# End pass over Wo by even and odd heads, eight projections in halves, two loads held back, in a two-layer memory-attention and gated-MLP kernel

## The chip, the cores and the metric

The kernel runs on one core of a Trainium2 chip. The metric is the device time of one execution in microseconds. A core has a TensorE (PE) for matmuls, a VectorE (DVE), a ScalarE (ACT), a GpSimd (POOL) and a SyncE (SP), each with its own instruction queue, which it works through in order. DMAs are issued from the queues of SP and POOL here. Matmul results go to PSUM banks of 512 fp32 columns on 128 partitions.

## The reference, cut to what matters

```python
x = A_x                                                  # (1, 2048, 512)
x = x + _A_ref(_layernorm(x), A_mem0, A_Wq, A_Wk, A_Wv, A_Wo, 32)
x = x + _B_ref(_layernorm(x), B_w_in, B_w_sp, B_b_sp, B_w_out)
x = x + _A_ref(_layernorm(x), A_mem0, A_Wq, A_Wk, A_Wv, A_Wo, 32)
x = x + _B_ref(_layernorm(x), B_w_in, B_w_sp, B_b_sp, B_w_out)

def _A_ref(x, mem0, Wq, Wk, Wv, Wo, seg_len):            # 64 segments of 32 tokens, 32 heads of 128
    mem, outs = mem0, []
    for s in range(n_seg):
        h = concatenate([mem, x[:, 32*s:32*s+32]])       # 8 memory rows + 32 tokens
        q, k, v = h @ Wq, h @ Wk, h @ Wv
        p = softmax(where(mask, q @ k.T * scale, -1e9))
        o = (p @ v) @ Wo                                 # summed over the heads
        mem = o[:, :8]                                   # into the next segment
        outs.append(o[:, 8:])
    return concatenate(outs)

def _B_ref(x, w_in, w_sp, b_sp, w_out):                  # w_in (512, 1376), w_sp (2048, 2048)
    z = gelu(x @ w_in)
    z1, z2 = z[..., :688], layernorm(z[..., 688:])
    g = w_sp @ z2 + b_sp
    return (z1 * g) @ w_out
```

## The kernel before, in words

Weights and activations are bf16, sums fp32. Each of the two layers is an `a_block` (attention) followed by a `b_block` (gated MLP). Rows of x are handled in 16 tiles of 128.

**a_block.** 64 segments run one after the other, since the memory rows of one feed the next. `segment(s, ...)` computes Q, K and V of the segment's 32 rows. A matmul uses 32 of the array's 128 columns, so four of them, at column strips 0, 32, 64 and 96 (`tile_position`), run side by side (L689, L879). Scores (L903), probabilities times V (L929), and sums over keys (L975, L984) follow; then `wo_pass` (L746) applies Wo to give the next memory rows. `uT` holds the attention result that goes into Wo for the next pass: results of a segment's first 24 tokens are put through Wo one segment later together with the next segment's memory rows. The last 8 tokens of each segment (`oB`) go through Wo in groups of 16 segments, later, in `y_part`/`wo_last` (L759, matmuls of 512 columns, four strips), and are added into `yB` by VectorE (L776). Each segment calls back: `fill()` for such extra TensorE work, `spare1` and `spare2` for row work in the middle, `tail` at the end.

The number of TensorE instructions in a segment is kept constant by splitting some projections in two (`pads_of`): `PE_PAGE = 256` and three pages per segment.

**The last segments (60 to 63).** The MLP's weights w_in are loaded into the `front` buffer in four slices (`load_w(kt)`, L169 and L170, two DMAs of 176 KB each, issued from POOL). `front` also holds attention buffers of even row tiles, so a slice may be loaded once TensorE has read those. Rows that are finished are joined with x (`y_load` L220 and L222, `y_add` L226, `y_stats`, `y_norm` L236), stored as x (`xd`) and, normalised, as `xb_d`; `load_rows` (L177) brings them back transposed for the MLP. Tile 11's rows are loaded into `rowsB` in segment 63's `spare1`.

**The end pass.** After segment 63, the last segment's tokens (`uT`) and the last 8 tokens of tile 15's four segments (`oB`) still have to go through Wo: the loop at L1111 to L1116. For each of 32 heads, four matmuls of 256 columns: strips 0 and 1 take `uT` with the lower and upper half of Wo's columns, strips 2 and 3 the same with `oB`. ACT copies the bank's 256 columns (L1118), and four DMAs store it (L1123, L1125), two from SP and two from POOL. ACT then loads the Gelu table.

**b_block.** `project(tt)` for 16 row tiles (12 matmuls each in three column chunks, L282, into `pz`, of which there are two), Gelu on ACT (L283), row statistics on VectorE (L286); meanwhile rows of tiles 12 to 15 are joined (`late_sum`, `late_norm`). Then `gate` (L383) over w_sp, `product`, `finish` (L426).

PE, DVE and ACT run in the order in which the code is written (`manual_schedule`, which in `b_block` includes SP). In `a_block`, the instructions of POOL and SP are put in order by a scheduler that places each by when its inputs are ready; a load that nothing holds back can so be placed ahead of the point where it is written. Before, slice 2 of w_in is written in segment 62's `tail` and issued at the start of segment 61, and tile 11's o_d rows are written in segment 63's `spare1` and issued in segment 61.

Of the kernel before, what the change touches and what calls it, by code (L numbers as in the profile page):

```python
# [8 lines left out]
F32 = mybir.dt.float32  # L9
ACT = mybir.ActivationFunctionType  # L10
ALU = mybir.AluOpType
# [3 lines left out]
P = 128  # L15
DM = 512
KT = 4
H = 32
DH = 128
HD = H * DH  # L20
M = 8
SEG = 32
LN_EPS = 1e-5
FF = 1376
FH = 688
# [214 lines left out]
def b_block(tc, c, rows, front, xd, MV_out, RS_out, w_sp, w_out, S, first, ahead, wo, out_final=None):  # L240

    nc = tc.nc
    NT = S // P
    ident_bf = c["ident_bf"]
    with ExitStack() as ctx:
# [17 lines left out]
        def z(tt, lo=0, hi=FF):  # L263
            return zs[tt >= 6][:, tt - 6 * (tt >= 6), lo:hi]
# [12 lines left out]
        def project(tt):  # L277
            pz = big.tile([P, 1536], F32, name="pz")
            xnT = front.xnT[tt // 2][:, :, P * (tt % 2):P * (tt % 2) + P]
            for c0, c1 in ((0, 512), (512, 1024), (1024, FF)):  # L280
                for kt in range(KT):
                    nc.tensor.matmul(pz[:, c0:c1], lhsT=xnT[:, kt, :], rhs=w_in_sb[:, kt, c0:c1], start=(kt == 0), stop=(kt == KT - 1))  # L282
            nc.scalar.activation(out=z(tt), in_=pz[:, 0:FF], func=ACT.Gelu_apprx_tanh)  # L283
            st = zp.tile([P, 2, nc.vector.BN_STATS_DIM], F32, name="bnst2")
            for k in range(2):
                nc.vector.bn_stats(out=st[:, k, :], in_=z(tt, 344 * k, 344 * k + 344))  # L286
            nc.vector.bn_aggr(out=slot(tt), in_=st[:])

        def slot(tt):
            group = next(g for g in GROUPS if tt in g)  # L290
            if group not in where:
                where[group] = (zp.tile([P, 8, 2], F32, name="mv"), zp.tile([P, 8], F32, name="rs"), zp.tile([P, 8], F32, name="nb"))
            return where[group][0][:, group.index(tt), :]
# [31 lines left out]
        for k in range(4):  # L325
            if k == 0:
                x, o = (rows.pool.tile([P, DM], F32, name=name)[:] for name in ("y_x", "y_o"))
                spare = x.bitcast(BF16)
            elif k == 1:
                x, o = (gp.tile([P, DM], F32, name="xo")[:] for _ in range(2))  # L330
            else:
                wl = wsp_pools[k - 1].tile([P, 2, DM], F32, name="wspL", tag="wspT")
                x, o = wl[:, 0, :], wl[:, 1, :]
# [38 lines left out]
        n = 6 * P  # L372
# [260 lines left out]
def a_block(tc, c, rows, front, MV_in, RS_in, MV_out, RS_out, ahead, wo, S, first):  # L633
    nc = tc.nc
    NSEG = S // SEG
    NB = S // P
# [3 lines left out]
    with ExitStack() as ctx:  # L640
# [13 lines left out]
        wk = ctx.enter_context(tc.tile_pool(name="a_work", bufs=2))  # L654
# [44 lines left out]
        o_d, maskM = rows.o_d, c["maskM"]  # L699
# [7 lines left out]
        rowsB = rowp.tile([P, 2, 512], BF16, name="rowsB", bufs=1)  # L707
        copies, turns, adds = [], [], []

        def run(todo):  # L710
            while todo:
                todo.pop(0)()
# [50 lines left out]
        def y_part(G, q, last=False):  # L763

            groups = [oBs[G][:, :, 32 * g:32 * g + 32] for g in range(4)]
            if last:
                parts = [[(groups[g], 8 * q + k) for g in range(3)] + [(groups[q], 24 + k)] for k in range(8)]
            else:
                parts = [[(groups[g], 8 * q + k) for g in range(4)] for k in range(8)]
            pwB = accA.tile([P, DM], F32, name="pwB")  # L770
            for k, _ in enumerate(wo_last(parts, pwB)):
                if k + 1 in (1, 2, 4):
                    yield

            def add(lo, n, src):
                nc.vector.tensor_tensor(out=yB[G][lo:lo + n, :], in0=pwB[src:src + n, :], in1=yB[G][lo:lo + n, :], op=ALU.add)  # L776

            def out():
                n = 96 if last else P
                if q == 0:  # L780
                    yB[G] = wk.tile([P, DM], F32, name="yB", bufs=1)
                    nc.vector.tensor_copy(yB[G][0:n, :], pwB[0:n, :])
                else:
                    add(0, n, 0)
                if last:
                    if q == 2:
                        store_last(G, 0, 64, nc.sync)
                    add(32 * q, 32, 96)
                    if q == 2:
                        store_last(G, 64, 96, nc.sync)  # L790
                elif q == 3 and G < NB // 4 - 2:
                    stores.append(lambda: store_last(G, 0, P, nc.sync))
                elif q == 3:
                    store_last(G, 0, P, nc.sync)

            adds.append(out)
            yield
# [240 lines left out]
        def values(units):  # L1038
            for n in (3, 1):
                for _ in range(n):  # L1040
                    next(units)
                run(copies)
                yield

        for s in range(NSEG):
            tb, j4 = s // 4, s % 4
            if j4 == 0:
                q = tb % 4
                more = y_part(tb // 4 - 1, q) if tb > 3 else iter(())
            if first and s == 0:  # L1050
                more = values(units)
            if j4 > 0 and tb == NB - 1:
                more = y_part(tb // 4, j4 - 1, last=True)
            elif j4 == 1:
                more = b_units(tb + 1)
            if j4 == 1 and tb + 2 < NB:
                rows.load(tb + 2, first, nc.sync)

            def spare1():
                if first and s == 1:  # L1060
                    ln_turn(1)
                if ys:
                    rows.y_add(ys[0], first, nc.vector, nc.sync)
                elif stores:
                    last = yB[tb // 4 - 1][:, 0:1]
                    nc.vector.tensor_copy(last, last)
                    run(stores)
                if j4 == 3 and tb + 2 < NB:
                    rows.apply(tb + 2, MV_in, RS_in, first=first)
                if s == NSEG - 1:  # L1070
                    rows.y_load(due[0], first, nc.sync, rows.pool.tile([P, DM], F32, name="y_x")[:],
                                rowsB[:].rearrange("p a n -> p (a n)").bitcast(F32))()

            def spare2():
                if first and s == 0:
                    rows.apply(1, MV_in, RS_in, first=True)
                if first and s == 8:
                    c["cast_bsp"] = c["load_bsp"]()
                if first and s == 12:
                    c["cast_bsp"]()  # L1080
                if ys:
                    y_stats(ys[0])
                if j4 == 2 and tb + 2 < NB and first:
                    _stats(nc, rows.pool, rows.xs[tb + 2], MV_in[:, tb + 2, :])
                    copies.append(lambda: _rstd_act(nc, RS_in[:, tb + 2:tb + 3], MV_in[:, tb + 2, 1:2], c))

            def tail():
                if j4 == 0 and tb + 1 < NB and not (first and s == 0):
                    ln_turn(tb + 1)
                if tb == NB - 1:  # L1090
                    front.load_w(j4)
                    if j4 > 0:
                        front.load_rows(j4 - 1)
                if ys:
                    y_norm(ys.pop(0), nc.sync)
                if tb % 4 == 3 and j4 == (tb + 1 < NB) and tb > 4:
                    due.extend(range(tb - 7, tb - 3))

                if due and (j4 != 3 or tb + 2 >= NB) and s < NSEG - 1:
                    ys.append(due.pop(0))  # L1100
                    rows.y_load(ys[0], first, nc.sync)()

            segment(s, lambda: next(more, None), spare1, spare2, tail)
# [4 lines left out]
        y_norm(due[0], nc.sync)  # L1108
        ends = (uT[NSEG % 2], oBs[NB // 4 - 1][:, :, 96:128])
        pw = accB.tile([P, 512], F32, name="pw")  # L1110
        for h in range(H):  # L1111
            n = h // 8 * 8 + 2 * (h % 4) + h // 4 % 2
            for k in range(4):
                nc.tensor.matmul(pw[32 * k:32 * k + 32, 0:256], lhsT=ends[k // 2][:, n, :],
                                 rhs=wo.head(h).rearrange("p (kt g el) -> p g kt el", kt=4, g=4)[:, k % 2 * 2:k % 2 * 2 + 2],
                                 start=(h == 0), stop=(h == H - 1), tile_position=(0, 32 * k))  # L1116
        o_sb = wk.tile([P, 256], F32, name="o_end", bufs=1)
        nc.scalar.copy(o_sb[:], pw[:, 0:256])  # L1118
        for k in range(4):
            c0 = 256 * (k % 2)  # L1120
            eng = nc.sync if k % 2 else nc.gpsimd
            if k < 2:
                eng.dma_start(o_d[SEG * NSEG - 24:SEG * NSEG, c0:c0 + 256], o_sb[32 * k + 8:32 * k + 32, :])  # L1123
            else:
                eng.dma_start(o_d[M + P * NB - P:M + P * NB, c0:c0 + 256].rearrange("(j r) c -> j r c", j=4)[:, 24:32, :], o_sb[32 * k:32 * k + 32, :])  # L1125
        run(copies)
        _act_table(nc, GELU_SET)

# [34 lines left out]
```

## Time and profile before

| what | us |
|---|---|
| time, median of 4 runs (lowest to highest) | 1758.62 (1754.68 to 1759.27) |
| the profiled execution: its time | 1754.68 |
| the profiled execution: its span, first to last instruction | 1753.0 |
| end pass, layer 1: first matmul to first projection | 755.88 to 760.00 |
| end pass, layer 2 | 1611.37 to 1615.70 |
| tile 11's rows, layer 1: issue, VectorE's addition | 725.24, 758.02 |

The page gives, per engine, busy time and instructions; a chain of work followed back from the last instruction; groups of instructions by source line with mean duration; and idle time before a group with what ended it ("issue" where nothing in the profile shows it). Timelines list instructions by start in microseconds from the first instruction of the span, followed by duration, engine, line, operation, output and inputs, and a count where like instructions were merged. A waits view adds up the waits of one engine in a stretch: total us, number, longest. The trace also has every DMA packet with its queue, start and duration.

In this stretch view the columns are the stretch's length and each engine's busy time in it, TensorE's granted clock, the mean busy share of the 16 DMA engines, and what they moved:

```profile
720.30:732.80 12.50, 11.47 (x392) 8.79 (x392) 8.91 (x22) 7.45 (x16) 1.25 (x3) 1.00 0.42 132
732.80:744.30 11.50, 10.89 (x388) 8.46 (x384) 9.83 (x24) 7.56 (x18) 0.00 (x0) 1.00 0.26 78
744.30:755.90 11.60, 10.98 (x392) 8.63 (x392) 10.06 (x24) 7.95 (x19) 0.00 (x0) 1.00 0.25 78
755.90:760.00 4.10, 3.86 (x133) 3.35 (x125) 3.41 (x6) 0.33 (x2) 1.50 (x3) 1.00 0.38 109
```

The rows are segments 61, 62 and 63 of layer 1 and its end pass. Segment 61 is a microsecond longer than the two after it, and the DMA engines move most in it.

### The profile page before, as it was taken

What the parts mean: (1) busy time and instruction counts of PE and PEld (TensorE: products, weight loads), DVE (VectorE), ACT (ScalarE), POOL (GpSimd) and SP (SyncE); (2) the same over time, 40 slices, a digit from 0 to 9 for tenths busy, and PEclk for the clock granted to TensorE, in tenths of its full rate; (3) what the DMA queues carried; (4) which work ended last, traced back from release to release, by engine and by line L of the source; (5) the groups of instructions that cost most, each with busy time, mean ns of one, the idle gap of its engine ahead of it and who ended that gap; (6) DMA issues with size and microseconds to landing.
All of it is one profiled execution on the core that took longest, in us unless ns stands there. A gap on an engine that the chain in (4) does not pass through costs nothing.

```text
span 1753.0 us, 109803 instructions
## 1 busy us (share of the span) xinstructions
PE 1689.0 (96%) x51174; PEld 1268.5 (72%) x51174; DVE 1164.3 (66%) x2872; ACT 1110.2 (63%) x2274; POOL 121.8 (7%) x274
## 2 busy tenths in 40 slices
PE   2999999999999999999999999999999999999999
PEld 1677777777777777756667777777777777777565
DVE  2566677778777866785366666666776677667722
ACT  1677777777777777662047777777777777776500
POOL 6000000000000000021100000000000000001100
PEclk9999999999999999999999999999999999999999
DMA  9201000012001201267950000000210022114687
GB/s 351 72 20 20 21 20 18 20 48 68 20 21 50 72 24 38 76 169 147 205 165 23 24 23 24 24 23 24 77 59 24 23 81 62 32 33 136 152 186 167
DMA packets 191962, 124.54 MB, mean 71 GB/s; under 512 B 135976, under 2 KB 168200, under 8 KB 191504
## 3 DMA queue, kind: packets, MB, share of 16 engines
q1 hardware_dynamic: 182800, 90.37, 21.3%
q0 software_dynamic: 8688, 27.14, 4.8%
q8 instruction: 400, 6.55, 1.6%
q14 instruction: 58, 0.48, 0.1%
q10 hardware_dynamic: 16, 0.01, 0.0%
HBM read 57.06 MB, written 33.53 MB: 52 GB/s over the span
## 4 chain that ended last, share of the span: by engine, by line
PE 93%; DMA 3%; DVE 1%; issue 1%; POOL 1%; ACT 0%; SPq 0%; DVEq 0%; POOLq 0%
PE psV L689 14%; PE psm L689 14%; PE pw L746 13%; PE psm L879 13%; PE psb L689 9%; PE pg L383 7%; PE psS L903 5%; PE psO L929 4%; PE pz L282 4%; PE pwB L759 3%; PE py L426 2%; PE psD L984 2%; PE psM L975 2%; DMA Wo_high<-in_A_Wo_dram 1%; DMA Wv_sb<-in_A_Wv_dram 1%
## 5 line engine op out<-in xcount | busy, mean ns | idle before, releaser
L689 PEld LDWEIGHTS <-hA 128*32 128x32 bf16 x10964 | 356.5, 96 | 156.5 <-DVE hA L820 54.5
L689 PE MATMUL psV<-Wv_sb,hA 128*32 128x256 bf16 (+1 forms) x5795 | 282.7, 318 | 2.2 <-issue 1.8
L746 PEld LDWEIGHTS <-uT 128*32 128x32 bf16 x16384 | 232.0, 97 | 48.1 <-DVE uT L996 41.4
L879 PEld LDWEIGHTS <-hA 128*32 128x32 bf16 x8192 | 237.0, 97 | 0.7
L866 ACT CAST rows<-psm 128x512 bf16<-128x512 f32 x256 | 149.8, 585 | 135.4 <-PE psm L689 135.4
L943 DVE TENSOR_TENSOR uT<-psO,Rt 128x384 bf16<-128x384 f32 x256 | 140.7, 550 | 111.7 <-ACT Rt L1002 111.6
L882 ACT CAST rows<-psm 128x256 bf16<-128x256 f32 x512 | 191.0, 374 | 16.8
L910 ACT ACTIVATE E<-psS 128x448 bf16<-128x448 f32 x256 | 125.6, 541 | 116.6 <-PE psS L903 116.4
L996 DVE TENSOR_TENSOR uT<-psO,Rm 128x128 bf16<-128x128 f32 x256 | 62.5, 286 | 163.3 <-PE psO L929 163.3
L1002 ACT ACTIVATE Rt<-Rt 128x512 f32<-128x512 f32 x256 | 157.4, 629 | 4.0
L383 PE MATMUL pg<-z,wspT 128*128 128x344 bf16 x1024 | 154.4, 309 | 0.3 <-DMA wspT<-in_B_w_sp_dram 0.3
L689 PE MATMUL psm<-Wk_sb,hA 128*32 128x256 bf16 (+1 forms) x3121 | 144.6, 307 | 8.6 <-issue 5.4
L746 PE MATMUL pw<-Wo_high,uT 128*32 128x128 bf16 x8704 | 145.6, 219 | 1.7 <-DMA Wo_high<-in_A_Wo_dram 1.7
L689 PE MATMUL psm<-Wq_sb,hA 128*32 128x512 bf16 x2048 | 134.0, 382 | 8.3 <-DVE hA L820 8.0
L746 PE MATMUL pw<-Wo,uT 128*32 128x128 bf16 x7680 | 135.5, 219 | 4.1 <-DVE uT L996 3.0
L383 PEld LDWEIGHTS <-wspT 128*128 128x128 bf16 x1024 | 100.1, 98 | 53.7 <-DMA wspT<-in_B_w_sp_dram 0.6
L879 PE MATMUL psm<-Wk_sb,hA 128*32 128x256 bf16 x4096 | 136.7, 273 | 0.0
L879 PE MATMUL psm<-Wq_sb,hA 128*32 128x256 bf16 x4096 | 136.7, 273 | 0.0
L994 ACT ACTIVATE Rt<-psD 128x1024 f32<-128x1024 f32 x128 | 128.9, 1007 | 0.0
L913 DVE TENSOR_TENSOR E<-E,maskN 128x448 bf16<-128x448 bf16 x256 | 104.2, 409 | 36.9 <-ACT E L910 34.8
L689 PEld LDWEIGHTS <-hB 128*32 128x32 bf16 x2976 | 82.9, 97 | 53.3 <-DVE hB L604 26.9
L870 DVE STREAM_TRANSPOSE QQ<-rows 128x512 bf16<-128x512 bf16 x128 | 88.9, 694 | 34.3 <-ACT rows L866 34.3
(171 smaller groups left out, 2753.5 us busy)
## 6 DMA issues: line engine op xcount, KB each, us to landing
o_d<-o_sb SPq DMA_DIRECT2D x126, 64.0 KB
ln_x<-xd SPq DMA_DIRECT2D x26, 256.0 KB
y_o<-o_d SPq DMA_DIRECT2D x22, 256.0 KB
xd<-y_o SPq DMA_DIRECT2D x22, 256.0 KB
y_x<-xd SPq DMA_DIRECT2D x22, 256.0 KB
Wq_sb<-in_A_Wq_dram POOLq DMA_DIRECT2D x8, 512.0 KB, 6.9
Wk_sb<-in_A_Wk_dram POOLq DMA_DIRECT2D x8, 512.0 KB, 10.2
Wv_sb<-in_A_Wv_dram POOLq DMA_DIRECT2D x8, 512.0 KB, 11.5
```

Of the source, the lines that this page charges most:

```text
L383: nc.tensor.matmul(pg[t][:, k, 0:344], lhsT=wsp[t][:, st, :], rhs=z(st, 344 * k, 344 * k + 344), start=(st == 0), stop=(st == NT - 1))
L689: nc.tensor.matmul(o, lhsT=lhs(kt, cg), rhs=r, start=(kt == 0 and a == 0), stop=(kt == KT - 1 or halved > 0), tile_position=(0, 32 * cg), ...
L746: nc.tensor.matmul(po[32 * cg:32 * cg + 32, 0:128], lhsT=lhs[:, n, :], rhs=wo_rhs(h, cg), start=(h == 0), stop=(h == H - 1), tile_position ...
L866: nc.scalar.copy(r[:], ps[:])
L870: nc.vector.transpose(out=QQ[:, j % 2, :, 0:32] if j < 2 else KA[:, j % 2], in_=r[:])
L879: nc.tensor.matmul(ps[32 * cg:32 * cg + 32, 0:256].rearrange("p (i c) -> p i c", i=2), lhsT=hA_cur[:, kt, :], rhs=qk_rhs(w, j, kt, cg)[:, ...
L882: nc.scalar.copy(r[:, 256 * a:256 * a + 256], ps[:, 0:256])
L910: nc.scalar.activation(out=E[:, r], in_=pS, func=ACT.Exp, scale=scale)
L913: nc.vector.tensor_tensor(out=E[:, r], in0=E[:, r], in1=maskN[:, j4, :].unsqueeze(1).to_broadcast([P, 4, 112]), op=ALU.mult)
L943: nc.vector.tensor_tensor(out=hview(uT_nxt[:], r, 8, 32), in0=oview(r, 8, 32), in1=r_view(r)[:, :, :, 0:24], op=ALU.mult)
L994: nc.scalar.activation(out=Rt[:], in_=psD[:], func=ACT.Ln)
L1002: nc.scalar.activation(out=rt, in_=rt, func=ACT.Exp, scale=-1.0)
```

## The change

Four edits. In the end pass, matmuls take all 512 columns: strips 0 and 2 handle even heads, strips 1 and 3 odd heads, 16 steps of four, so each result stands as two partial sums. ACT copies the whole bank, VectorE adds each odd partial sum (from the copy) to the even one (from PSUM), and two DMAs store the sums. In layer 1's projections of tiles 8 to 15, the first two column chunks of 512 are done as two of 256 each. A memset by VectorE of two columns of w_in's slice 2 is written in segment 62's `spare1`, the slice's load follows it there, and `tail` leaves it out. A memset by VectorE of one column of `rowsB` is written ahead of tile 11's load in segment 63.

```diff
@@ project
-            for c0, c1 in ((0, 512), (512, 1024), (1024, FF)):
+            edges = (0, 256, 512, 768, 1024, FF) if first and tt >= NT // 2 else (0, 512, 1024, FF)
+            for c0, c1 in zip(edges, edges[1:]):
                 for kt in range(KT):
                     nc.tensor.matmul(pz[:, c0:c1], lhsT=xnT[:, kt, :], rhs=w_in_sb[:, kt, c0:c1], start=(kt == 0), stop=(kt == KT - 1))
@@ spare1
+                if s == NSEG - 2:
+                    nc.vector.memset(front.w_in_sb[:, 2, FH - 1:FH + 1], 0.0)
+                    front.load_w(2)
                 if s == NSEG - 1:
+                    nc.vector.memset(rowsB[:, 0, 0:1], 0.0)
                     rows.y_load(due[0], first, nc.sync, ...)()
@@ tail
                 if tb == NB - 1:
-                    front.load_w(j4)
+                    if j4 != 2:
+                        front.load_w(j4)
@@ the end pass
-        for h in range(H):
-            n = h // 8 * 8 + 2 * (h % 4) + h // 4 % 2
+        for i in range(H // 2):
             for k in range(4):
-                nc.tensor.matmul(pw[32 * k:32 * k + 32, 0:256], lhsT=ends[k // 2][:, n, :],
-                                 rhs=wo.head(h).rearrange("p (kt g el) -> p g kt el", kt=4, g=4)[:, k % 2 * 2:k % 2 * 2 + 2],
-                                 start=(h == 0), stop=(h == H - 1), tile_position=(0, 32 * k))
-        o_sb = wk.tile([P, 256], F32, name="o_end", bufs=1)
-        nc.scalar.copy(o_sb[:], pw[:, 0:256])
-        for k in range(4):
...
+                h = 2 * i + k % 2
+                n = h // 8 * 8 + 2 * (h % 4) + h // 4 % 2
+                nc.tensor.matmul(pw[32 * k:32 * k + 32, :], lhsT=ends[k // 2][:, n, :], rhs=wo.head(h).rearrange("p (kt g el) -> p g kt el", kt=4, g=4),
+                                 start=(i == 0), stop=(i == H // 2 - 1), tile_position=(0, 32 * k))
+        o_sb = wk.tile([P, DM], F32, name="o_end", bufs=1)
+        nc.scalar.copy(o_sb[:], pw[:])
+        for k in range(2):
+            o = o_sb[64 * k:64 * k + 32, :]
+            nc.vector.tensor_tensor(out=o, in0=pw[64 * k:64 * k + 32, :], in1=o_sb[64 * k + 32:64 * k + 64, :], op=ALU.add)
+            if k == 0:
+                nc.gpsimd.dma_start(o_d[SEG * NSEG - 24:SEG * NSEG, :], o[8:32, :])
             else:
+                nc.sync.dma_start(o_d[M + P * NB - P:M + P * NB, :].rearrange("(j r) c -> j r c", j=4)[:, 24:32, :], o)
```

In the changed program VectorE's and ACT's orders are as before but for the added instructions. On POOL, slice 2's two DMAs move behind the last QQ copy (L813), with nothing between them and the end pass's loads. On SP, tile 11's o_d load moves from behind tile 8's to behind tile 11's own x load (y_x); the instructions that it passes keep their order. The loads of tiles 12 to 15 on POOL change places among themselves around the end pass's store. TensorE's 102,348 matmul and weight-load instructions become 102,220: 128 fewer in each end pass, 128 more in layer 1's projections.

More of the change, by code (lines that the diff above doesn't have):

```diff
@@ L1110, in a_block @@
         pw = accB.tile([P, 512], F32, name="pw")
-        for h in range(H):
-            n = h // 8 * 8 + 2 * (h % 4) + h // 4 % 2
+        for i in range(H // 2):
             for k in range(4):
-                nc.tensor.matmul(pw[32 * k:32 * k + 32, 0:256], lhsT=ends[k // 2][:, n, :],
-                                 rhs=wo.head(h).rearrange("p (kt g el) -> p g kt el", kt=4, g=4)[:, k % 2 * 2:k % 2 * 2 + 2],
-                                 start=(h == 0), stop=(h == H - 1), tile_position=(0, 32 * k))
-        o_sb = wk.tile([P, 256], F32, name="o_end", bufs=1)
-        nc.scalar.copy(o_sb[:], pw[:, 0:256])
-        for k in range(4):
[L1120 to L1123, printed above, removed]
+                h = 2 * i + k % 2
[9 more added lines that the diff above has]
+                nc.gpsimd.dma_start(o_d[SEG * NSEG - 24:SEG * NSEG, :], o[8:32, :])
             else:
-                eng.dma_start(o_d[M + P * NB - P:M + P * NB, c0:c0 + 256].rearrange("(j r) c -> j r c", j=4)[:, 24:32, :], o_sb[32 * k:32 * k + 32, :])
+                nc.sync.dma_start(o_d[M + P * NB - P:M + P * NB, :].rearrange("(j r) c -> j r c", j=4)[:, 24:32, :], o)
         run(copies)
```

## The prediction

> **What bounds the kernel now.** I read the page's busy row and chain first, then the DMA queues, then PE's waits at the place the change touches, then the timelines there.
>
> ```profile
> PE 1689.0 (96%) x51174; PEld 1268.5 (72%) x51174; DVE 1164.3 (66%) x2872; ACT 1110.2 (63%) x2274; POOL 121.8 (7%) x274
> PEclk9999999999999999999999999999999999999999
> q8 instruction: 400, 6.55, 1.6%
> PE 93%; DMA 3%; DVE 1%; issue 1%; POOL 1%; ACT 0%; SPq 0%; DVEq 0%; POOLq 0%
> ```
>
> TensorE is the chain (93%), at full clock, so only what TensorE does or waits for counts. The third line matters more than its 1.6%: 400 packets of 16 KB are instructions. TensorE has 102,348 of the 109,803, and 102,348/400 is 256 per packet: q8 carries TensorE's stream, one packet per 256 instructions. Counting instructions from the start, every large "issue" gap in the attention segments falls on the same place modulo 256, so these are page boundaries. For 30 boundaries before the first end pass I set the trace's q8 packet against TensorE's crossing: the packet mostly starts 1.0 to 1.2 us after the previous crossing (later where bulk transfers run), takes 0.9 to 1.4, and TensorE runs on 1.2 to 1.6 us after its end. Together some 3.6 us, and an undisturbed segment (10.79 us, three pages) consumes a page in 3.60. The fetch has no slack: whatever delays its packet stops TensorE.
>
> ```profile
> PE psm L689 <- DVE yB L776: 1.2, 2, 0.6
> PE psV L689 <- issue: 0.9, 1, 0.9
> PE pw L1114 <- issue: 0.2, 1, 0.2
> PE pw L746 <- issue: 0.2, 1, 0.2
> ```
>
> These are TensorE's waits from 700 to 760 us (total, times, longest): all that can go in the last segments of layer 1. The "issue" rows are the fetch. In the timelines:
>
> ```profile
> 725.46 0.39 PE L689 MATMUL psV<-Wv_sb,hA 128*32 128x512 bf16 x2
> 726.70 1.02 PE L689 MATMUL psV<-Wv_sb,hA 128*32 128x512 bf16 x16 [0.85 <-issue]
> ...
> 720.07 0.54 POOL L169 DMA_DIRECT2D front<-in_B_w_in_dram  x1 [5.26 <-PE pwB L759]
> 720.72 0.54 POOL L170 DMA_DIRECT2D front<-in_B_w_in_dram  x1
> ...
> 720.21 0.51 SPq L826 DMA_DIRECT2D o_d<-o_sb  x1
> 721.17 0.56 SPq L752 DMA_DIRECT2D o_d<-yB  x1
> ```
>
> Segment 61 starts at 720.3. Four transfers (352 KB of w_in's third slice, 64 KB, 256 KB) are issued before page boundary 721.85; their packets run from 721.3 to 724.3, and the q8 packet starts at 724.28, 2.44 us after the crossing instead of 1.1. TensorE stands still from 725.46 to 726.70. Layer 2 has the same picture (gap 1.38 at 1582.46).
>
> ```profile
> 756.75 0.28 PE L1114 MATMUL pw<-Wo,uT 128*32 128x256 bf16 x2
> 757.27 0.29 PE L1114 MATMUL pw<-Wo,old 128*32 128x256 bf16 x2 [0.24 <-issue]
> ...
> 760.00 9.47 PE L282 MATMUL pz<-front 128*128 128x512 bf16 x48
> ```
>
> The end pass holds a boundary too: it runs 755.88 to 760.00 (4.12 us) and 1611.37 to 1615.70 (4.33).
>
> **The change part by part** (against the profiled execution: span 1753.0, its time 1754.68).
>
> *End pass.* 128 matmuls of 256 columns become 64 of 512. Each of the four column strips still streams 32x256 = 16x512 = 8192 columns, so halving the count saves hardly any streaming: groups of four 256s start 0.109 us apart (32x0.109 = 3.49), groups of four 512s in L759 0.2155 apart (16x0.2155 = 3.45). What goes is the boundary stall: the boundary lies 68 instructions in, reached after 34 matmuls; at the new pace that is 1.83 us in instead of 0.9, while the page is ready about 1.5 us in. Gain 4.12-3.45 = 0.67 and 4.33-3.45 = 0.88.
>
> *Its way out.* The copy is 128x512 (0.585 us by L866, was 0.364) and two VectorE adds of 32x512 follow (0.69 each by L776), behind tile 11's y_norm. Four stores become two. The later store leaves about when the last of four did (762.5), so POOL's load behind it (769.15, waiting for o_end) stays; the reordering of POOL's other late loads shifts them by some 0.5 us, and the additions that use them begin at 767.3. Cover: ACT's copy, table load (1.28) and first Gelu (1.32) end near 763.4, and the third projection wants its bank at about 764.05: 0.4 us left after the semaphore. The rows of tile 15 are not used before project(14) at 792.5. Cost 0; if the cover were short, 0.2 per layer.
>
> *Split projections.* Layer 1, tiles 8 to 15: 64 matmuls more. L412's 256-column matmuls with full 128x128 weights start 109.2 ns apart, L282's 512s 215.9: 2.5 ns each, +0.16 us, on the path (TensorE waits for nothing there). Its 128 instructions replace those of the end pass, so layer 2 keeps its page places, but for one of two wait instructions in layer 1's gating (L383) that drops out. That moves layer 2's boundaries by one instruction; segments average 11.14 us in layer 1 and 11.11 in layer 2, which stand one instruction apart for the most part today, so I take 0, ends -2 and +2 over the layer.
>
> *Third slice of w_in held.* A VectorE memset after segment 62's y_add (at about 740.65) now releases it. POOL has nothing queued behind it until the end pass, project(0) needs it at 760: cover 15 us. Gone in segment 61: 1.24 less some 0.1 that its row stores leave = 1.14; layer 2 1.38-0.1 = 1.28. New in segment 62: SP issues 256 KB (740.64) and 128 KB (741.01; 256 KB in layer 2), POOL the 352 KB at 740.75, all before boundary 742.31. The segment-61 stack moved 672 KB in 3.0 us; 736 KB from 741.7 ends near 744.5, so the packet that started at 743.05 starts near 744.5. Before, its boundary (746.66) had 0.9 us spare, because TensorE had waited 0.8 us for yB's adds (the L776 row). Remaining stall 0.4; layer 2, with 128 KB more and less spare, 0.7. Ends 0 (the packet slips between, as at 708.26, 0.3 late amid the fourth slice) and 1.3 each. I take the segment-61 stack, being nearest.
>
> Here the Trainium skill speaks against the change. "Runtime: NRT & Kernel Launch", section "Instruction fetch mechanics", says a page boundary costs one queue-tail bump, mostly hidden, since fetching runs ahead of issue. By it both hold-backs are worth nothing, and I would count only the end pass: -1.55+0.16 = -1.4. The trace has 1.24 and 1.38 us of standstill ended by exactly that packet; I count them. "DMA: Bandwidth & Descriptors", "Issuing engines are not separate DMA queues", says transfers from all engines share the same 16 DMA engines: moving a load does not remove its bytes. That agrees with 0.4 and 0.7 above rather than 0.
>
> *Tile 11's rows held.* The load moves in SP's queue from 725.24 to behind segment 63's y_x (752.55), to about 753.0; behind it stand o_sb's store (755.53) and yB's stores (756.82), untouched. At the old place the boundary after (730.73) had a gap of 0.39: gain 0.3 in layer 1, 0 in layer 2 (0.11). At the new place 256 KB join the packets of 752.9 to 754.5 just as the fetch of 754.66 is due, which feeds the end pass's boundary: about 0.7 late against 0.35 spare plus the gap between: 0.1 in layer 1, 0.4 in layer 2 where y_x is double. Ends 0 and 0.8.
>
> *Sum.* Layer 1: -0.67-1.14-0.3+0.4+0.1+0.16 = -1.45. Layer 2: -0.88-1.28+0.7+0.4 = -1.06. Together **-2.5 us**: 1752.2 against 1754.68. The profiled execution is the fastest of four; the median is 1758.62, so I forecast 1756.1.
>
> **Rivals.**
> 1. *The stall only moves.* The held slice stops TensorE in segment 62 as it did in 61 (1.2 each), tile 11's rows 0.5 each. For it: a like stack of bytes at a like distance before a boundary; against: the 0.8 us wait for yB just there. -2.72-1.55+0.16+2.4+1.0 = -0.7: 1757.9.
> 2. *The new places cost nothing.* For it: fetch packets do slip between w_in packets (708.26). -2.72-1.55+0.16 = -4.1, with a little more if one-instruction phases help: 1754.
> 3. *Slower: tile 11's rows come late.* VectorE's y_add of tile 11 (758.02), its statistics, ACT's RS, end copy, table load and first Gelu are one chain in queue order; it decides from a landing after about 758.4, and then every us costs one us per layer. At the old place such a load took 2.5 us from issue to its last packet (725.24 to 727.74); here it has 5.4. Behind a full queue, 7.5 us would give +2.1 per layer: -2.5+4.2 = +1.7, 1760.3.
>
> **How the numbers follow.** Forecast (gain 1 to 4) 0.52, rival 1 0.13, rival 2 0.20, rival 3 with an unlucky phase 0.15. 0.2% is 3.5 us, about what a measurement tells from none. Faster by more: rival 2 and 0.22 of the forecast, 0.42; slower by more: most of rival 3, 0.12; the rest 0.46. The forecast alone spans 1754.6 to 1757.6; adding the four runs' scatter (about 2 us each way) and the ends of the unknown costs, 1751.8 to 1760.2.
>
> **What would show it.** Right: the 1.2 us gap in segment 61 gone; the end pass near 3.5 us; segment 62 longer by 0.4 to 0.7; 256-column projections 109 ns apart. Wrong: gaps over 1 us in segment 62 or 63, a wait of project(2) for ACT, or attention segments of layer 2 that differ throughout.

## The result, and the profile after

The changed kernel takes 1756.44 us (median of 43 runs, 1751.37 to 1764.54); the kernel before took 1760.53 (64 runs, 1754.68 to 1770.37) beside it. The ratio is 0.9976, 95% interval 0.9969 to 0.9984: **4.2 us faster, between 2.8 and 5.5**. The forecast of 2.5 us faster had the direction, but lies just outside the interval: the sum was too small. That its absolute figure, 1756.1, is only 0.3 us from the median is luck, since the kernel before took 1.9 us more in this comparison than in the four runs the forecast started from. The profiled execution took 1751.82 us, its span is 1750.1, 2.9 less than before.

From the page of the changed kernel, the busy row, the instruction queue and the chain by engine:

```profile
PE 1688.9 (96%) x51110; PEld 1271.7 (73%) x51110; DVE 1167.3 (67%) x2880; ACT 1110.9 (63%) x2274; POOL 120.8 (7%) x272
q8 instruction: 399, 6.54, 1.6%
PE 93%; DMA 3%; DVE 2%; issue 1%; POOL 1%; ACT 0%; SPq 0%; DVEq 0%; POOLq 0%
```

TensorE is still the chain and as busy as before. There is one instruction packet less; that proves to matter below. Line numbers have moved with the added lines: L689 is L690 here, and the end pass's L1114 is L1121. The waits of TensorE from 700 to 757 us, the last segments of layer 1 (total, times, longest):

```profile
PE psm L690 <- DVE yB L777: 1.2, 2, 0.6
PE psm L690 <- issue: 0.6, 1, 0.6
PE psV L690 <- issue: 0.2, 1, 0.2
```

The wait ahead of `psV` in segment 61 fell from 0.9 to 0.2 and the one in the end pass is gone. The new one, `psm` 0.6, is segment 60's: slice 3 of w_in, which the change leaves alone, meets a boundary there in this execution (before, it did so in layer 2 alone). The stretches of segments 61, 62, 63 and the end pass, columns as in the table shown of before:

```profile
719.05:730.45 11.40, 11.23 (x392) 8.72 (x390) 8.88 (x22) 7.42 (x16) 0.40 (x1) 1.00 0.32 91
730.45:742.05 11.60, 10.98 (x392) 8.51 (x391) 9.85 (x25) 7.66 (x18) 1.06 (x2) 1.00 0.34 108
742.05:753.60 11.55, 10.93 (x392) 8.53 (x392) 10.04 (x25) 7.89 (x19) 0.00 (x0) 1.00 0.33 101
753.60:757.20 3.60, 3.60 (x69) 1.81 (x62) 3.27 (x6) 0.03 (x1) 1.60 (x3) 1.00 0.33 79
```

Segment 61 is down from 12.50 to 11.40 and the end pass from 4.10 to 3.60, while 62 and 63, which took over the DMA traffic (78 GB/s before, now 108 and 101), took as long as before (11.60 and 11.54 us against 11.59 and 11.54, by the table of stages below). What is left in segment 61 shows in TensorE's timeline and SP's:

```profile
724.20 0.39 PE L690 MATMUL psV<-Wv_sb,hA 128*32 128x512 bf16 x2
724.77 0.83 PE L690 MATMUL psV<-Wv_sb,hA 128*32 128x512 bf16 x14 [0.17 <-issue]
```

```profile
718.95 0.51 SPq L827 DMA_DIRECT2D o_d<-o_sb  x1
719.92 0.55 SPq L753 DMA_DIRECT2D o_d<-yB  x1
```

From 724.20 to 724.77 only two matmuls start: a gap of 0.56 us between starts, where it was 1.24. The two row stores (64 and 256 KB) stand ahead of this boundary as before. In the packet records the boundary before was crossed (the first matmul of its page started) at 720.59, the store's last packets leave at about 722.5, and the q8 packet starts at 722.49, 1.90 us after the crossing. Undisturbed it starts after 1.0 to 1.2.

**Where the time went, by stage.** The stages are measured from first matmul to first matmul; "gaps" are the distances between the starts of the last matmul before a page boundary and the first after it, summed over the boundaries of segments 1 to 59.

| us | before | after |
|---|---|---|
| layer 1: segments 60, 61, 62, 63 | 11.38, 12.47, 11.59, 11.54 | 11.55, 11.40, 11.60, 11.54 |
| layer 1: end pass, projections | 4.12, 37.18 | 3.59, 37.34 |
| layer 1: gating | 103.26 | 102.88 |
| layer 2: segments 60, 61, 62, 63 | 11.54, 12.33, 11.59, 11.54 | 11.53, 11.40, 11.59, 11.78 |
| layer 2: end pass, projections | 4.33, 37.18 | 3.85, 37.68 |
| layer 2: gating to the end | 100.10 | 99.02 |
| segments 1 to 59 without gaps, layers 1 and 2 | 633.6, 632.3 | 633.4, 631.8 |
| gaps of segments 1 to 59, layers 1 and 2 | 21.2, 20.9 | 20.0, 23.3 |

The stages that the prediction's sum is about gave 1.26 us in layer 1 and 0.68 in layer 2. A further 1.08 came from layer 2's gating and end, about which the prediction said nothing. Layer 1's gating gave 0.38 (0.3 us is a wait for `w_sp` that this profile no longer has; experiment 7 has it again at 0.2, so the gain is not shown to be the change's), and segments 1 to 59 without their gaps 0.7: 4.1 us in all. The gaps of segments 1 to 59 differ by chance from execution to execution: the changed kernel, profiled a second time, had 60.5 us of them in place of 43.3 and a span of 1767.0. Without these gaps the spans are 1710.9 before and 1706.8 and 1706.5 after. That difference, 4.1 to 4.4 us, agrees with the ratio of the runs.

### The profile page after: what moved, and what is told of

Its sections match the earlier page's. It is cut to its first block, busy times and chain, and to the rows that moved or that the text cites. A ratio compares the mean times of both kernels' runs of the same rounds, so it can differ in the third digit from the quotient of the medians.

```text
span 1750.1 us, 109678 instructions
## 1 busy us (share of the span) xinstructions
PE 1688.9 (96%) x51110; PEld 1271.7 (73%) x51110; DVE 1167.3 (67%) x2880; ACT 1110.9 (63%) x2274; POOL 120.8 (7%) x272
## 4 chain that ended last, share of the span: by engine, by line
PE 93%; DMA 3%; DVE 2%; issue 1%; POOL 1%; ACT 0%; SPq 0%; DVEq 0%; POOLq 0%
PE psV L690 14%; PE psm L690 14%; PE pw L747 13%; PE psm L880 13%; PE psb L690 9%; PE pg L384 8%; PE psS L904 5%; PE psO L930 4%; PE pwB L760 3%; PE pz L283 3%; PE py L427 2%; PE psD L985 2%; PE psM L976 2%; DMA Wo_high<-in_A_Wo_dram 1%; DMA Wv_sb<-in_A_Wv_dram 1%
## 5 line engine op out<-in xcount | busy, mean ns | idle before, releaser
L690 PEld LDWEIGHTS <-hA 128*32 128x32 bf16 x10964 | 356.3, 96 | 152.8 <-DVE hA L821 54.0
L690 PE MATMUL psV<-Wv_sb,hA 128*32 128x256 bf16 (+1 forms) x5795 | 281.6, 318 | 0.7 <-issue 0.5
L690 PE MATMUL psm<-Wk_sb,hA 128*32 128x256 bf16 (+1 forms) x3121 | 144.1, 307 | 8.1 <-issue 4.5
L690 PE MATMUL psm<-Wq_sb,hA 128*32 128x512 bf16 x2048 | 134.0, 382 | 8.2 <-DVE hA L821 7.8
L914 DVE TENSOR_TENSOR E<-E,maskN 128x448 bf16<-128x448 bf16 x256 | 104.2, 409 | 40.2 <-ACT E L911 37.9
L690 PEld LDWEIGHTS <-hB 128*32 128x32 bf16 x2976 | 82.1, 97 | 51.1 <-DVE hB L605 24.2
```

Source lines behind the costliest of these rows:

```text
L690: nc.tensor.matmul(o, lhsT=lhs(kt, cg), rhs=r, start=(kt == 0 and a == 0), stop=(kt == KT - 1 or halved > 0), tile_position=(0, 32 * cg), ...
L914: nc.vector.tensor_tensor(out=E[:, r], in0=E[:, r], in1=maskN[:, j4, :].unsqueeze(1).to_broadcast([P, 4, 112]), op=ALU.mult)
```

## The experiments

Ten further kernels ran, one of them the changed kernel again. Times are set against the kernel before on the same chip. One execution's span scatters by some 15 us through the gaps of segments 1 to 59, so the readings below go by the stages of one profiled execution each. Two numbers together are those of layers 1 and 2.

**1. The end pass and the splits alone, both loads where they were** (edit against the changed kernel).

```diff
-                if s == NSEG - 2:
-                    nc.vector.memset(front.w_in_sb[:, 2, FH - 1:FH + 1], 0.0)
-                    front.load_w(2)
...
-                    nc.vector.memset(rowsB[:, 0, 0:1], 0.0)
...
-                    if j4 != 2:
-                        front.load_w(j4)
+                    front.load_w(j4)
```

> The end pass and the split projections alone, both loads where they were. Fetch theory: the end passes fall from 4.12 and 4.33 us to about 3.5 to 3.6, with no gap at their page boundary; segment 61 keeps its gap of 1.2 to 1.4 us in both layers. Time 1.0 to 1.4 us under the kernel before. Rival (page fetches cost nothing, the end pass is all there is): all of the measured 4 us are here.

Ratio 0.9982 (0.9970 to 0.9995). That is not told apart from the whole change's 0.9976, so by the time alone the rival stands; the stages, and experiment 4, speak against it. The end pass took 3.56 and 4.00 us (in layer 2 a gap of 0.44 stayed at its boundary), segment 61 12.75 and 12.90 (its boundary's gap 1.25 and 0.97). So the end pass's gain of 0.56 and 0.33 needs no hold-back, and segment 61's stall does not go without one. Layer 2's gating with its end took 99.03, as in the whole change: that gain belongs to this part. Without the gaps of segments 1 to 59 its span is 1709.3 us, between the 1710.9 of the kernel before and the 1706.8 of the changed one.

**2. Slice 2 held back alone**, in the kernel before.

```diff
+                if s == NSEG - 2:
+                    nc.vector.memset(front.w_in_sb[:, 2, FH - 1:FH + 1], 0.0)
+                    front.load_w(2)
...
-                    front.load_w(j4)
+                    if j4 != 2:
+                        front.load_w(j4)
```

> Only w_in's slice 2 is held until segment 62. Fetch theory: segment 61 falls from about 12.4 to about 11.4 to 11.6 us in both layers, its gap from 1.2 to 1.4 us to 0.4 to 0.6 (yB's row store is still ahead of the packet); segment 62 stays within 0.3; the end passes stay above 4 us. Time 1.4 to 1.9 us under the kernel before. Rival (the stall only moves): segment 62 grows by about 1 us in each layer and the time is that of before.

Ratio 0.9995 (0.998 to 1.001). Segment 61 lost its stall (11.54 and 11.92 us, the boundary's gap 0.60 and 0.42), but the gap at segment 63's first boundary grew from 0.09 to 0.32 and 0.50, and the old end pass took 4.54 and 4.74 in place of 4.12 and 4.33. Segments 61 to 63 and the end pass together took 40.1 and 40.2 us, and 39.7 and 39.8 in the kernel before: what one boundary gained, others gave back, and the 1.4 to 1.9 us that were expected do not show. The loss is in segment 63 and the end pass, not in segment 62 as the rival has it. Whether the hold-back lengthened the end pass is not shown, because that boundary's gap differs between executions.

**3. Tile 11's rows held back alone**, in the kernel before.

```diff
                 if s == NSEG - 1:
+                    nc.vector.memset(rowsB[:, 0, 0:1], 0.0)
```

> Only tile 11's rows are held until segment 63. Fetch theory: the gap of 1.2 to 1.4 us in segment 61 stays, since the load was issued after its packet; the next boundary's gap of 0.39 in layer 1 goes; the old end pass, which has no spare at its boundary, gets a longer gap there (0.4 to 1 us more) in layer 2 and perhaps in layer 1. Time 0 to 1 us slower than before. Rival (the hold is worth what the diff suggests): 0.5 us faster.

Ratio 0.9991 (0.9978 to 1.0003). Segment 61's boundary kept a gap of 0.98 and 1.11 us, and the next one's 0.39 in layer 1 went. The old end pass took longer, 4.75 and 4.80. Its waits in layer 2:

```profile
PE pw L1115 <- issue: 0.9, 1, 0.9
```

The load now stands ahead of the instruction packet for the boundary inside the end pass, and the gap there is 1.15 and 1.19 us where it was 0.51 and 0.72. How much of that is the load's is not shown: experiment 2, with the rows where they were, had 0.94 and 1.14 there. The new end pass reaches its boundary some 0.9 us later; with the same load ahead of it, the gap was 0.02 and 0.28 in the changed kernel, and 0 to 0.17 in layer 1 and 0 to 0.90 in layer 2 in the profiles of experiments 5, 6, 7, 9 and 10. So the new end pass mostly hides the load, but not in every execution.

**4. The change without the split projections.** The sum held the splits to cost 0.16 us; this was to show whether they do anything else.

```diff
-            edges = (0, 256, 512, 768, 1024, FF) if first and tt >= NT // 2 else (0, 512, 1024, FF)
+            edges = (0, 512, 1024, FF)
```

> The whole change but for the split projections, so that layer 2's page boundaries lie 128 instructions elsewhere in every segment. If the place of the boundaries matters: layer 2's segments 1 to 59 take 3 us or more longer than the 653 to 655 of the two traces, and the time is at or over the kernel before. If it does not: the same 653 to 655 and a time 0.2 us under the changed kernel's (ratio about 0.9975).

Ratio **1.0303 (1.0272 to 1.0335)**: 1825.65 us against 1768.43, 57 us slower by the medians and 54 by the ratio. Layer 1's projections fell by the 0.16 us, and layer 2's segments 1 to 59 rose from 655 to 716 us. TensorE's waits in those segments, first in the changed kernel and then in this one:

```profile
PE psm L690 <- DVE hA L821: 3.0, 4, 0.7
PE psm L690 <- issue: 2.2, 4, 1.1
...
PE pw L747 <- issue: 0.6, 2, 0.4
```

```profile
PE pw L747 <- issue: 64.5, 59, 2.3
PE psm L690 <- DVE hA L821: 2.9, 4, 0.7
```

One wait of about 1.1 us in each of the 59 segments, inside `wo_pass`. One of them in the timeline, with the idle time before it in brackets:

```profile
1212.69 0.67 PE L747 MATMUL pw<-Wo_high,uT 128*32 128x128 bf16 x34
1214.59 0.40 PE L747 MATMUL pw<-Wo_high,uT 128*32 128x128 bf16 x14 [1.23 <-issue]
```

With 128 instructions fewer, layer 2's boundaries lie half a page from where they were. The reader can see why that matters from the work in each page, taken as the time from one crossing to the next less the gap (medians): 3.60, 3.64 and 3.46 us for a segment's three pages in the changed kernel, but 4.16, **2.20** and 4.40 here. A page's fetch takes some 3.6 us, so the page of 2.2 stops TensorE for about 1.4, and the other two cannot give it back: 59 x 1.4 = 83, measured 79.1 us of gaps, 77.4 of them at the end of that page. That is 1.31 us each, so for a short page the fetch is nearer 3.5 us than 3.6.

**5. Six of the eight projections split**, to move layer 2's boundaries by 32 instructions only.

```diff
-            edges = (0, 256, 512, 768, 1024, FF) if first and tt >= NT // 2 else (0, 512, 1024, FF)
+            edges = (0, 256, 512, 768, 1024, FF) if first and tt >= NT // 2 + 2 else (0, 512, 1024, FF)
```

> The changed kernel with six of the eight layer-1 projections split (32 PE instructions fewer), so that every page boundary of layer 2 lies 32 instructions later in its segment. Page theory: each boundary falls max(0, 3.6 us minus the page's own work) late; over the work times of the changed kernel's trace that is 23 us in layer 2's segments 1 to 59 where the changed place gives 5 us (and 79 us was got with all splits gone). So layer 2's segments 1 to 59 take 665 to 675 us in place of 655, and the whole is 10 to 20 us slower than the changed kernel (ratio to before 1.003 to 1.009). Rival, only the full half page is bad, by something else in that kernel: layer 2 within 3 us of the changed kernel's 655.

A miss: ratio 0.9987 (0.997 to 1.0003), layer 2's segments 660.3 us, which is within what the changed kernel itself shows (655.2 and 668.1 in two executions). The pages' work here is 3.81, 3.19 and 3.77 us. For the page of 3.19 a fetch of 3.6 asks for 24 us of gaps (59 x 0.41); 16.5 were measured, 0.28 each, which again makes the fetch some 3.5 us. The other two pages, with 0.3 us of slack, had 8.7. The changed kernel has 23.3 us of gaps, where the expectation counted 5: 12.7 at the end of its page of 3.46, and 10.6 at the other two, where no gap is due and only late or long packets can make one. So the expectation took the fetch too long and the gaps it started from too small; 25.4 us in all stand against 23.3. A shift of 32 instructions cost nothing that can be told from the scatter; half a page cost some 55 us.

**6. The changed kernel again**, on one chip with the next kernels.

> The changed kernel once more, so that its ratio stands beside those of its parts on one chip. Parts measured so far: end pass with splits 0.9982, slice 2 held alone 0.9995, tile 11's rows held alone 0.9991; their product is 0.9968. Parts add up: 0.997 (0.9955 to 0.9985), about 5 us off. If the holds collide with each other or with the new end pass: 0.9985 or above. In the profile: the stall of segment 61's boundary stays at 0.4 to 0.7 us in both layers, because the row store still goes ahead of that instruction packet.

Ratio 0.9986 (0.9962 to 1.001), too wide to tell the two cases apart. Segment 61's gaps were 0.42 and 0.42, within what was expected. But segment 63 took 11.91 and 12.65 us, where the first profile has 11.54 and 11.78: in layer 2 its boundaries have gaps of 0.51 and 0.69. The packet for the first of these had started 2.40 us after the crossing, behind the held slice. This execution's span was 1767.0 us, and TensorE's waits in layer 2's segments 1 to 59 begin with

```profile
PE psm L690 <- issue: 6.1, 17, 0.8
```

against 2.2 in four waits in the first profile. The view lists only the larger ones; all gaps of both layers are 60.5 against 43.3 us. That 17.2 is the whole difference between the two spans (16.9).

**7. Slice 3 held back as well**, from segment 60 to segment 61's `spare1`.

```diff
+                if s == NSEG - 3:
+                    nc.vector.memset(front.w_in_sb[:, 3, FH - 1:FH + 1], 0.0)
+                    front.load_w(3)
...
-                    if j4 != 2:
+                    if j4 < 2:
```

> The changed kernel with slice 3 of w_in held as well, from segment 60 to segment 61's spare1. Fetch theory: the stall of 0.8 us in segment 60 in both layers was slice 3's transfer ahead of an instruction packet; it goes (0 to 0.3 us left), and the transfer's new place is before the boundary from segment 61 to 62, which has 0.9 us of slack from the wait for yB: segment 60 falls from 11.5 to about 10.8 us in each layer, 0.5 to 1.5 us less in all than the changed kernel (ratio to before lower by 0.0003 to 0.0009). Rival, the stall only moves: segments 60 to 62 together unchanged (within 0.2 us), segment 61 or 62 longer by what segment 60 loses.

Segment 60 fell to 10.79 and 10.83 us in both layers, as the fetch theory had it. In layer 2, segments 60 to 62 together fell from 34.52 to 33.82; in layer 1 they stayed (34.57 against 34.55), for 61 and 62 became 0.3 and 0.5 longer. Ratio 0.9980 (0.9963 to 0.9997), not told apart from the changed kernel's. In experiment 6 layer 1's segment 60 took 10.90 without this hold, so that stall does not occur in every execution.

**8. Slice 2 released one segment later**, beside tile 11's rows.

```diff
-                if s == NSEG - 2:
+                if s == NSEG - 1:
                     nc.vector.memset(front.w_in_sb[:, 2, FH - 1:FH + 1], 0.0)
```

> The changed kernel with slice 2 released one segment later, in segment 63, beside the load of tile 11's rows. Place theory: two transfers (256 KB each) now stand ahead of the packet for the boundary inside the end pass, so the stall there grows from 0.03 and 0.28 us to 0.8 to 1.5 us in each layer; segment 62 falls by 0 to 0.3. Rival, the place of a held transfer does not matter: stages 60 to 63 and the end pass within 0.3 us of the changed kernel's.

This kernel has one execution and so no ratio. The end pass took 4.94 and 4.90 us (changed kernel 3.59 and 3.85), and the gap at its boundary was 1.38 and 1.34. TensorE's waits there, the same row in both layers:

```profile
PE pw L1121 <- issue: 1.0, 1, 1.0
```

The q8 packet started 2.66 and 2.63 us after the crossing, where the changed kernel has 1.42 and 1.73. The place of a held transfer decides; the rival falls. (The slice is 352 KB, not the 256 of the expectation, and segment 62 did not fall: 11.90 and 11.61 us.)

**9. Layer 2's projections split too**, which puts its gating's boundaries back where they lay before.

```diff
-            edges = (0, 256, 512, 768, 1024, FF) if first and tt >= NT // 2 else (0, 512, 1024, FF)
+            edges = (0, 256, 512, 768, 1024, FF) if tt >= NT // 2 else (0, 512, 1024, FF)
```

> The changed kernel with layer 2's projections of tiles 8 to 15 split as well, which puts the 128 instructions back that layer 2's end pass lost, so that the page boundaries of layer 2's gating lie again where they lay before. Page theory: TensorE's idle of about 0.5 us ahead of L427 comes back in layer 2, the instruction packets are 400 in place of 399, and layer 2's gating with its end takes 99.5 to 100.1 us in place of 99.02; its projections take 37.34 in place of 37.18. Rival, layer 2's gating became shorter for another reason (the reordered last loads, the lighter way out): it stays at 99.0.

This kernel, too, has one execution. There were 400 packets again, and layer 2's gating with its end took 100.07 us. The first group of `finish` in layer 2, in the timelines of the kernel before, the changed kernel, and this one:

```profile
1667.76 1.47 PE L426 MATMUL py<-w_out_sb,front 128*128 128x512 bf16 x6 [0.53 <-DMA front<-front]
```

```profile
1665.28 1.46 PE L427 MATMUL py<-w_out_sb,front 128*128 128x512 bf16 x6
```

```profile
1683.95 1.47 PE L427 MATMUL py<-w_out_sb,front 128*128 128x512 bf16 x5 [0.86 <-DMA front<-front]
```

The idle time went with the boundary and came back with it. Over the twelve profiles, with two layers each, the boundary lies in this group 13 times, and each time TensorE stood idle 0.3 to 0.9 us ahead of the group; the other 11 times it did not. In experiment 4, layer 1 has lost the boundary and the idle time, and layer 2 has both (0.56 us).

The profile names a DMA, not "issue": it is SP's transpose of `u`. VectorE's next product waits for the same transpose in this kernel, whereas in the changed one it waits for TensorE. So what is late is the transpose, and not TensorE's instructions:

```profile
1684.02 0.93 DVE L392 SCALAR_TENSOR_TENSOR front<-pg,bsp,z 128x688 bf16<-128x688 f32 x1 [1.72 <-DMA front<-front]
```

```profile
1665.48 0.93 DVE L392 SCALAR_TENSOR_TENSOR front<-pg,bsp,z 128x688 bf16<-128x688 f32 x1 [0.82 <-PE pg L384]
```

The packet records show what goes with a boundary. In this kernel the transpose's data packets end at about 1681.4, the q8 packet runs from 1680.96 to 1682.13, and of the transpose's last 32 packets of 4 bytes, 30 leave by 1681.5 but two at 1682.8; TensorE starts at 1683.95. In layer 1 of the changed kernel, where the boundary has not moved (idle 0.86), 30 leave by 807.2 and the last two at 808.01, just when the q8 packet ends (807.01 to 808.02). In its layer 2, without a boundary there, all 32 leave by 1663.8. So an instruction packet can hold up a data transfer's end, as a data transfer holds up an instruction packet; by what path is not shown.

**10. Slice 3 held, and layer 1's 128 extra instructions taken from its gating's last two tiles** in place of its projections, so that layer 1's gating also loses that boundary. The edit that holds slice 3 is that of experiment 7 and is left out.

```diff
-            edges = (0, 256, 512, 768, 1024, FF) if first and tt >= NT // 2 else (0, 512, 1024, FF)
+            edges = (0, 512, 1024, FF)
...
-                    nc.tensor.matmul(pg[t][:, k, 0:344], ...)
+                    for lo, hi in ((0, 172), (172, 344)) if first and t >= NT - 2 else ((0, 344),):
+                        nc.tensor.matmul(pg[t][:, k, lo:hi], ...)
```

> The changed kernel with slice 3 held too (as in the run before) and the 128 extra PE instructions of layer 1 taken from its gating's last two tiles (344 columns as 2 x 172) in place of its projections. Gating theory: TensorE's idle 0.5 to 0.9 us ahead of the first group of L427 appears where a page boundary lies in that group, and not elsewhere; here layer 1's boundary leaves it, so layer 1's gating loses that idle and falls from 102.7 by 0.3 to 0.9 us (if 172-column matmuls run at their columns' pace), its projections from 37.34 to 37.18, and layer 2 keeps its page places (segments 1 to 59 at 655 to 668 us, not 716). In all 0.5 to 1 us less than with slice 3 held alone (ratio to before about 0.997 to 0.998). Rival, the idle belongs to layer 1's traffic and not to the boundary: the gating stays at 102.7 or above.

Ratio 0.9978 (0.9962 to 0.9994). No idle time is left ahead of that group in layer 1; the gating took 102.40 us against 102.73 in experiment 7 (where the idle was 0.3) and 102.88 in the changed kernel (0.86). Experiments 4 and 5, whose layer 1 has no boundary in that group either, have 102.12 and 101.84. The projections are back at 37.18 and layer 2's segments 1 to 59 took 658 us. In layer 2 of this execution segment 61 took 13.20 us, because TensorE waited 2.0 us for `uT`, behind a row load that VectorE waited 3.1 us for; one profile does not say whether the edit has a part in it. Without the gaps of segments 1 to 59 its span is 1704.7 us, the lowest of all, against 1706.8. By its ratio it is not told apart from the changed kernel, so a version that beats it is not shown.

## Why the prediction was right in direction and too small

*The bound and the sum.* The bound was right: at full clock, most of what changed did so through page boundaries or what they touch. The stages that the sum counts gave 1.26 + 0.68 = 1.9 us, less than its 2.5; the other half of the measured 4.2 comes from places that it took at nothing. That the forecast is no further off is partly luck, since the two errors have opposite signs.

*End pass.* The sum had -0.67 and -0.88; measured -0.53 and -0.48. The matmuls run at the pace taken, and the boundary is reached late enough. What remains is tile 11's load ahead of it, which the prediction counted apart (0.1 and 0.4); the two terms together were -0.57 and -0.48, close in both layers. In layer 2 that is partly luck, with a gap that was 0 to 0.90 us in other executions (experiment 3).

*Slice 2 gone from segment 61.* The term "1.24 less some 0.1 that its row stores leave" was mis-sized. The stores leave 0.56 in both layers, since the packet waits for the 256 KB of `yB` to its last byte. The gain was 0.68 and 0.82 us, not 1.14 and 1.28. In the other profiles with this hold-back and the new end pass, 0.2 to 0.7 us were left in the layers whose page boundaries lie as here.

*Its new place in segment 62.* Taken at 0.4 and 0.7 from "the segment-61 stack, being nearest"; measured 0 and 0.24 in the first profile. The packet did start late (1.82 and 2.18 us after the crossing), but the slack from the wait for `yB` covered it in layer 1 wholly. In the second profile of the same kernel it was 0 and 0.42, and 0 to 0.44 in the other experiments that hold the slice there with the new end pass. So the lower end was nearest, and the value taken does occur. Layer 1's segment 61 also lost the 0.39 gap at its next boundary, as predicted (-0.3).

*Tile 11's rows and the way out.* Tile 11's rows cause no late addition. But a new wait of 0.3 us for a transposed tile appeared ahead of layer 2's thirteenth projection, tile 12's (the projections took 37.68 in place of 37.18). It belongs to the way out, whose loads of tiles 12 to 15 the prediction took at no cost. Experiment 8 has it too (37.75), the other seven profiles with the new end pass have not, so that the new order of the loads causes it is not shown.

*Splits.* +0.16 us was right to the hundredth, in layer 1. The sentence "its 128 instructions replace those of the end pass, so layer 2 keeps its page places" was right and unpriced: it was worth some 55 us (experiment 4). But it holds for layer 2's segments only. **The step that was missing** is that layer 2's own end pass also loses 128 instructions, with no splits to replace them, so that layer 2's gating moves by half a page. That took a packet away, and the step to the first matmul of `finish` fell from 0.84 to 0.15 us (0.53 us of idle time). The rest of the 1.08 us lies after the last matmul: 3.32 us pass from its end to the end of the span in the three profiles with the old end pass and 2.94 in the nine with the new one, splits in layer 2 or not. Its cause is open.

*The one-instruction shift.* Taken as 0, ends -2 and +2. Layer 2's segments 1 to 59 without their gaps take 632.1 to 632.3 us in the three kernels with the old end pass and 631.4 to 631.8 in the seven with the new one whose layer 2 lies at the changed kernel's place. Some 0.6 us agrees with the shift, but no run moved one instruction alone.

*The rivals.* "The stall only moves" comes nearest to slice 2's hold-back without the new end pass (experiment 2), though the stall moved to other places than it says; it does not describe the whole change. "The new places cost nothing" came nearest in time, with 4.1, but by luck: one place cost 0.24, and the parts that it counts gave 1.9 us. "Tile 11's rows late" did not occur.

*The rule that spoke against the change*, from the Trainium skill ("Runtime: NRT & Kernel Launch", section "Instruction fetch mechanics"), has a page boundary mostly hidden. Here it is not: half a page of shift made the kernel some 55 us slower, although it has 128 instructions and 0.16 us of work less (experiment 4).

## What to carry to other kernels

Where TensorE's instruction stream is dense, count instructions as well as time: a page (256 here) must hold at least as much work as its fetch takes (some 3.5 us here), so equal work per page matters more than a few instructions more or less, and an edit that changes the count moves every boundary behind it, in later layers and stages too. A transfer that is held back should be released ahead of a boundary with slack, and its new place priced from that slack and not from the stack it came from. Two transfers held to one boundary stopped TensorE for 1.3 us there (experiment 8).

## What the runs showed of the hardware beyond that

- Most of the scatter between executions lies in the gaps at page boundaries. Over the profiles, spans ran from 1750.1 to 1768.9 us (without experiment 4), and the gaps at page boundaries in segments 1 to 59 from 42 to 61 us; span less gaps stayed within 1704.7 to 1712.8, and within 0.3 for the two profiles of the same kernel.
- An instruction packet that falls at the end of a data transfer goes with a late completion: 0.3 to 0.9 us of waiting for a transpose in the 13 layers whose boundary lay there, none in the 11 where it did not.
